# Decode attention with adaLN: softmax rows turned by VectorE instead of TensorE, the second batch's scores placed behind the first value product, and w1 loaded in two halves

## The chip, the core and the metric

One core of one Trainium2 chip. The metric is device time in microseconds (us) for one execution of the program; the median of three runs is given, and beside it the time of the one execution that the profiler recorded. Engines: PE (TensorE, matmuls; PEld is its weight load), DVE (VectorE), ACT (ScalarE), POOL (GpSimd), and SP (SyncE), which here issues nearly all transfers.

## What is computed

One decode step, 8 batches, one token each, width 512. A conditioning vector gives six modulations. The normalised and modulated token is projected to 32 query heads; groups of 4 heads share one of 8 key/value heads; only the last 2048 of 8192 cached positions count. The result goes through `wo`, a gated residual, a second modulated norm, and a squared-ReLU MLP of width 1792. All of it is f32.

```python
    scores = jnp.einsum("bhqd,bhkd->bhqk", q, k) * (Dh ** -0.5)
    p = _softmax(scores, axis=-1)
    o = jnp.einsum("bhqk,bhkd->bhqd", p, v)
    return (lambda x, *d: x.transpose(*d))(o, 0, 2, 1, 3).reshape(B, Sq, Hq * Dh) @ wo
...
x = A_x
mod = (_silu(c) @ w_mod).reshape(c.shape[0], 6, 1, -1)
sa, ca, ga, sb, cb, gb = (mod[:, 0], mod[:, 1], mod[:, 2], mod[:, 3], mod[:, 4], mod[:, 5])
h = _layernorm(x, axis=-1) * (1 + ca) + sa
x = x + ga * _A_ref(h, A_k_cache, A_v_cache, A_wq, A_wo)
h = _layernorm(x, axis=-1) * (1 + cb) + sb
x = x + gb * _B_ref(h, B_w1, B_b1, B_w2, B_b2)
return x
```

## The kernel before

**Loads.** Four slots in SBUF, each 128 partitions x 32 KB, hold whatever is being read from HBM: `w_mod` and `wq` first, then keys and values, then `wo`, `w1`, `w2`. One K or V load is 4096 KB: four of the eight key/value heads of one batch. The order is fixed by the list `loads` (L104 to L111): K(0,0), K(0,1), K(1,0), V(0,0), K(1,1), V(0,1), K(2,0), V(1,0), and so on: the keys run one batch ahead of the values. A load is issued on SP's queue as soon as a slot is given back by `done`, and `done` is called where the code that last read the slot stands. SP's queue is in order. Issue and use are therefore tied to the order of the PE program: `scores(b, t)` gives back a K slot, `weighted(b, t)` a V slot.

**Scores.** K arrives with positions on partitions. `turn` (L284) transposes it in place on DVE in 32x32 squares, four pieces of 128x2048 a slot. `scores` (L294) then runs 16 matmuls against `qb`, a table with each query in a block of its own (`fill`, L271), and gathers one batch's scores in a PSUM tile S of 128x512.

**Softmax.** `rows` copies S to SBUF on ACT (L306) and permutes its partition rows by 16 matmuls against slices of the identity (L310) into a second PSUM tile. `maximum` (L320) takes each partition's maximum on DVE; in `exponent` four small matmuls (L326) share it among the partitions of one head, DVE takes the minimum of the four negated results (L330), and ACT exponentiates with a running sum (L333). `divisor` adds the sums over partitions by a matmul (L345) and inverts (L347, `rz`). `spread` writes the scaled probabilities four times over (L355, ACT); `turn_p` transposes them by PE in four parts n = 0 to 3, using two PSUM tiles in turn (L365), and masks them into `pT` on DVE (L366).

**Values.** `weighted(b, t)` (L378) multiplies `pT` into a V slot with 32 matmuls; ACT copies the result out (L388); `gather` adds the heads' parts into `oT` (L396 to L407).

**Order.** The loop at L409 writes out the order for every engine by hand: the softmax of batch b-1 lies between the four turns of K(b,0). All engines run their own instructions in order and meet at semaphores. For each b: maximum, turn, exponent and gather, turn, divisor and spread, turn, two `turn_p`, turn, two `turn_p`, `scores(b,0)`, `weighted(b-1,0)`, the four turns of K(b,1), `scores(b,1)`, `rows(b)`, `weighted(b-1,1)`.

**End.** `wo` in three loads (16, 12 and 4 of its 32 rows) is multiplied at L453; residual and norm give `h2T` (L143); then `w1` (one load, L485, 4 chunks of 4 matmuls), squared ReLU, a turn (`rT`), `w2` (four loads, L505) and the output.

Of the kernel before, what the change touches and what calls it, by code (L numbers as in the profile page):

```python
# [18 lines left out]
def tile_adaln_cached_attention_mlp(  # L19
# [51 lines left out]
    def load(key):  # L71
# [19 lines left out]
        elif kind == "w1":  # L91
            pieces = [(0, w1.rearrange(r_kc, p=P))]
        else:
            v = w2.rearrange("(p c) n -> p c n", p=P)
            pieces = [(lo, v[:, lo:hi]) for lo, hi in ((0, 8), (8, 12), (12, 13), (13, 14))]
# [31 lines left out]
    ident = consts.tile([P, 2, P], F32, name="ident")  # L127
    make_identity(nc, ident[:, 0, :])
    one = ident[:, 0, :]
    nc.vector.tensor_copy(ident[:, 1, :], one)  # L130
# [42 lines left out]
    def scaled(xm, rstd, add, name):  # L173
# [36 lines left out]
    nc.gpsimd.memset(oT, 0.0)  # L210

# [56 lines left out]
    qrep_b = qrep.rearrange("p x c r b -> p (x c r) b")  # L268

    def fill(b):  # L270
        nc.vector.tensor_mul(  # L271
            qb[b % 2][:, :, :4],
            qrep_b[:, :, b, None].to_broadcast([P, 128, 4]),
            block[:, None, :].to_broadcast([P, 128, 4]),
# [5 lines left out]
    S_, S2_, NM_, PR_, RZ_, PT_, O_ = {}, {}, {}, {}, {}, {}, {}  # L280
# [5 lines left out]
    def scores(b, t):  # L286
# [3 lines left out]
        q = qb[b % 2].rearrange("p n z -> p (n z)")  # L290
# [12 lines left out]
    def rows(b):  # L303

        ss = work.tile([P, 512], F32, name="ss", tag="a")
        nc.scalar.copy(ss, S_.pop(b))  # L306
        S2_[b] = ps_s.tile([P, 4, P], F32, name="s2_ps")
        for a in range(4):
            for j in range(4):
                nc.tensor.matmul(  # L310
                    S2_[b][32 * j : 32 * j + 32, a, :],
                    one[:, a::4],
                    ss[:, P * j : P * j + P],
                    start=True,
                    stop=True,
                )

    def maximum(b):
        mx = work.tile([P, 1], F32, name="mx")
        nc.vector.tensor_reduce(mx, S2_[b].rearrange("p a n -> p (a n)"), axis=AX.X, op=ALU.max)  # L320
        NM_[b] = mx
# [230 lines left out]
```

## Time and profile before

| | |
|---|---|
| median of 3 runs | 400.16 us (399.04 to 400.53) |
| profiled execution | 397.71 us, of it 395.8 us from first to last instruction (the span) |
| mean granted clock of PE | 0.853 |
| busy: PE / DVE / ACT | 274.2 / 195.0 / 47.2 us |
| moved by DMA | 165.18 MB, mean 417 GB/s |
| chain that ended last | DMA 52%, PE 27%, DVE 18% |

The page cuts the span into 40 slices of 9.9 us. A digit is a busy share in tenths; GB/s is what the DMA engines moved in the slice. In a row of instructions the columns are start, duration, engine, line, operation, output<-inputs, shape and count, and in brackets the idle time ahead and what ended it. A row of the grouped view has total busy time, mean ns of one, and idle time with what ended most of it. A row of the DMA issues has the count, KB each and median us from issue to landing.

### The profile page before, as it was taken

The page shows a single profiled execution, that of the slowest core. Times are in us where ns is not written, and L with a number is a line of the kernel's source. Part 1 is how long each engine was busy: PE and PEld are TensorE (multiplying, and loading weights), DVE is VectorE, ACT ScalarE, POOL GpSimd, SP SyncE. Part 2 cuts the span into 40 slices and gives each one's busy share as a digit, 9 for nine tenths or more (in the row PEclk, how much of TensorE's full clock was granted, in tenths as well). Part 3 has the DMA queues.
Part 4 walks back from the last instruction along what each step waited for, and adds up shares of the span by engine and source line. Part 5 has one row for each costly group of instructions (what it writes and reads, how often), then busy time and mean ns, then how long its engine had stood idle before and what let it go on. Part 6 is the DMA issues. An engine that isn't in the chain of part 4 may idle for free.

```text
span 395.8 us, 5381 instructions
## 1 busy us (share of the span) xinstructions
PE 274.2 (69%) x2448; PEld 125.2 (32%) x2448; DVE 195.0 (49%) x186; ACT 47.2 (12%) x95; POOL 4.6 (1%) x11
## 2 busy tenths in 40 slices
PE   0445717859968596859695969596939685988664
PEld 0211301235343224333422343234313433354123
DVE  2320298299084908491848184819281847030022
ACT  1300100030030003000300030003000300032010
POOL 4000000000000000000000000000000000000000
PEclk9986758968986879998868979997888898989889
DMA  8999999998999999999999999999999999999993
GB/s 330 426 434 442 437 431 427 424 422 325 426 442 450 426 424 422 431 429 454 429 425 426 424 426 434 449 431 422 431 422 431 442 426 431 434 429 424 418 422 120
DMA packets 6711, 165.18 MB, mean 417 GB/s; under 512 B 792, under 2 KB 1056, under 8 KB 1312
## 3 DMA queue, kind: packets, MB, share of 16 engines
q1 hardware_dynamic: 6480, 164.69, 97.3%
q8 instruction: 19, 0.31, 0.3%
q10 hardware_dynamic: 144, 0.13, 0.1%
q14 instruction: 4, 0.03, 0.0%
q0 software_dynamic: 64, 0.01, 0.0%
HBM read 164.77 MB, written 0.07 MB: 416 GB/s over the span
## 4 chain that ended last, share of the span: by engine, by line
DMA 52%; PE 27%; DVE 18%; ACT 1%; issue 1%; DVEq 0%; ACTq 0%
DMA slot<-in_A_k_cache_dram 43%; PE s_ps L294 17%; DVE slot L284 17%; DMA slot<-in_B_w_dram 6%; DMA xc_in<-in_xc_dram 3%; PE o_ps L378 3%; PE t_ps L365 2%; PE m_ps L219 2%; PE t_ps L485 1%; PE t_ps L505 1%; PE s_ps L310 1%; ACT prd L355 0%; ACT ss L306 0%; PE m_ps L326 0%; DVE e_sb L149 0%
## 5 line engine op out<-in xcount | busy, mean ns | idle before, releaser
L284 DVE STREAM_TRANSPOSE slot<-slot 128x2048 f32<-128x2048 f32 x64 | 144.2, 2288 | 40.2 <-DMA slot<-in_A_k_cache_dram 40.2
L294 PE MATMUL s_ps<-slot,qb 128*32 128x512 f32 x512 | 121.1, 1092 | 49.6 <-DVE slot L284 48.5
L294 PEld LDWEIGHTS s_ps<-slot,qb 128*32 128x32 f32 x512 | 25.1, 135 | 123.0 <-issue 78.3
L378 PE MATMUL o_ps<-slot,pT 128*32 128x256 f32 x1024 | 59.0, 380 | 0.0
L378 PEld LDWEIGHTS o_ps<-slot,pT 128*32 128x32 f32 x1024 | 39.9, 111 | 24.0 <-issue 9.8
L365 PE MATMUL t_ps<-ident,prd 128*128 128x128 f32 x128 | 30.5, 416 | 21.2 <-ACT prd L355 20.6
L320 DVE TENSOR_REDUCE mx<-s_ps 128x1 f32<-128x512 f32 x8 | 5.5, 691 | 72.9 <-PE s_ps L310 72.9
L365 PEld LDWEIGHTS t_ps<-ident,prd 128*128 128x128 f32 x128 | 23.9, 216 | 25.7 <-ACT prd L355 24.7
L388 ACT COPY o_sb<-o_ps 128x256 f32<-128x256 f32 x16 | 6.0, 372 | 140.2 <-PE o_ps L378 140.2
L355 ACT ACTIVATE prd<-pr,rz 128x512 f32<-128x512 f32 x32 | 20.5, 711 | 17.9 <-DVE rz L347 17.9
L366 DVE TENSOR_TENSOR pT<-t_ps,m4r 128x512 f32<-128x512 f32 x32 | 20.9, 670 | 3.2 <-PE t_ps L365 2.5
L241 PE MATMUL t_ps<-slot,h1T 128*32 128x512 f32 x64 | 12.1, 922 | 9.8 <-DMA slot<-in_A_wq_dram 9.8
L306 ACT COPY ss<-s_ps 128x512 f32<-128x512 f32 x8 | 4.7, 585 | 106.5 <-PE s_ps L294 106.5
L310 PEld LDWEIGHTS s_ps<-ss,ident 128*32 128x32 f32 x256 | 7.0, 139 | 20.8 <-ACT ss L306 20.8
L310 PE MATMUL s_ps<-ss,ident 128*32 128x128 f32 x256 | 8.9, 279 | 5.7 <-ACT ss L306 5.7
L453 PE MATMUL s_ps<-slot,oT 128*32 128x512 f32 x64 | 9.0, 712 | 5.1 <-DMA slot<-in_A_wo_dram 5.1
L253 DVE STREAM_TRANSPOSE qT<-t_ps 128x512 f32<-128x512 f32 x2 | 1.4, 716 | 19.0 <-PE t_ps L241 18.9
L159 PE MATMUL m_ps<-xsum,sel 128*128 128x1 f32 x2 | 0.6, 362 | 14.1 <-DVE xsum L182 14.1
L326 PEld LDWEIGHTS m_ps<-mx,nident 128*128 128x128 f32 x64 | 7.7, 191 | 3.9 <-issue 2.5
L326 PE MATMUL m_ps<-mx,nident 128*128 128x1 f32 x64 | 8.4, 253 | 0.8 <-DVE mx L320 0.8
L241 PEld LDWEIGHTS t_ps<-slot,h1T 128*32 128x32 f32 x64 | 2.8, 159 | 18.8 <-issue 13.4
L219 PE MATMUL m_ps<-slot,cT 128*32 128x384 f32 x64 | 7.3, 625 | 0.0
(90 smaller groups left out, 93.0 us busy)
## 6 DMA issues: line engine op xcount, KB each, us to landing
slot<-in_A_k_cache_dram SPq DMA_DIRECT2D x16, 4096.0 KB, 22.2
slot<-in_A_v_cache_dram SPq DMA_DIRECT2D x16, 4096.0 KB, 26.3
slot<-in_A_wq_dram SPq DMA_DIRECT2D x2, 4096.0 KB, 31.9
slot<-in_w_mod_dram SPq DMA_DIRECT2D x2, 3072.0 KB, 14.0
slot<-in_A_wo_dram SPq DMA_DIRECT2D x1, 4096.0 KB, 22.2
slot<-in_B_w_dram SPq DMA_DIRECT2D x1, 3584.0 KB, 24.3
slot<-in_A_wo_dram SPq DMA_DIRECT2D x1, 3072.0 KB, 24.3
slot<-in_B_w_dram SPq DMA_DIRECT2D x1, 2048.0 KB, 25.7
```

Of the source, the lines that this page charges most:

```text
L219: nc.tensor.matmul(pm[i][32 * q : 32 * q + 32, : 3 * P].rearrange("p (m n) -> p m n", m=3), cT[:, kc, :], wm[:, 3 * i : 3 * i + 3, q, :], ...
L241: nc.tensor.matmul(pq[t][32 * x : 32 * x + 32, :], hT[:, kc, :], w[:, 2048 * t + 512 * x : 2048 * t + 512 * x + 512], start=(kc == 0), sto ...
L284: nc.vector.transpose(k, k)
L294: nc.tensor.matmul(S_[b][32 * x : 32 * x + 32, :].rearrange("p (j i) -> p j i", i=8), q[:, n : n + 32], k[:, :, c, :, x], start=(t == 0 an ...
L310: nc.tensor.matmul(S2_[b][32 * j : 32 * j + 32, a, :], one[:, a::4], ss[:, P * j : P * j + P], start=True, stop=True,)
L326: nc.tensor.matmul(pw[:, w : w + 1], nident[:, 32 * w : 32 * w + P], NM_[b], start=True, stop=True)
L355: nc.scalar.activation(d, pr[:, 4 * n : 4 * n + 4, :, None].to_broadcast([P, 4, 32, 4]), AF.Copy, scale=RZ_[b][0])
L365: nc.tensor.transpose(pp[:, P * i : P * i + P], d[:, i].rearrange("p i u -> p (i u)"), one)
L366: nc.vector.tensor_mul(PT_[b][:, 4 * n : 4 * n + 4, :].rearrange("p j (q x r) -> p (j q) x r", x=4, r=8), pp.rearrange("p (q x r) -> p q x ...
L378: nc.tensor.matmul(o[32 * g : 32 * g + 32], PT_[b][:, j, 64 * q + t : 64 * q + 64 : 2], v[:, 2 * q : 2 * q + 2, j, :], start=(j < 2), stop ...
L388: nc.scalar.copy(O_[b][:, t], o)
L453: nc.tensor.matmul(wo_ps[32 * (i % 4) : 32 * (i % 4) + 32, :], oT[:, i, :], slot(("wo", i // 16), D)[:, i % 16, :], start=(i < 4), stop=(i ...
```

## The change

- The partition rows of S are permuted by two square transposes on DVE (`s1`, `s2`) in place of ACT's copy and 16 matmuls. The permutation differs, so `qb`, `pT`, the masks and the order of the V rows follow it.
- The maximum is shared by DVE alone: into one column of a zeroed 128x32 tile, a square transpose, a maximum over four groups, a scaled broadcast, a square transpose back.
- `rows`, `maximum` and `exponent` of batch b follow each other directly behind `scores(b,1)`; `divisor` and `spread` stand behind the first turn of the next batch, and each pair of `turn_p` one turn sooner than before.
- For b = 1 alone `weighted(0,0)` stands ahead of `scores(1,0)`.
- `w1` is loaded by two DMAs of two chunks each.
- The sum over partitions uses a table `same` in place of `sel`.

```diff
         elif kind == "w1":
-            pieces = [(0, w1.rearrange(r_kc, p=P))]
+            v = w1.rearrange(r_kc, p=P)
+            pieces = [(0, v[:, :2]), (2, v[:, 2:])]
...
+    m16 = consts.tile([P, 4, 4, REP], F32, name="m16")
+    nc.vector.tensor_copy(m16, m4[:, None, :, None].to_broadcast([P, 4, 4, REP]))
+    own = consts.tile([P, 4, 8], F32, name="own")
+    nc.vector.tensor_reduce(own, one.rearrange("p (x q r) -> p x r q", x=4, q=4), axis=AX.X, op=ALU.add)
+    same = consts.tile([P, 4, 4, 8], F32, name="same")
+    nc.vector.tensor_copy(same, own[:, :, None, :].to_broadcast([P, 4, 4, 8]))
...
+    mx = consts.tile([P, 32], F32, name="mx")
+    nc.gpsimd.memset(mx, 0.0)
...
     def rows(b):
-        ss = work.tile([P, 512], F32, name="ss", tag="a")
-        nc.scalar.copy(ss, S_.pop(b))
-        S2_[b] = ps_s.tile([P, 4, P], F32, name="s2_ps")
-        for a in range(4):
-            for j in range(4):
-                nc.tensor.matmul(
-                    S2_[b][32 * j : 32 * j + 32, a, :], one[:, a::4], ss[:, P * j : P * j + P],
...
+        s1 = work.tile([P, 4, 16, 8], F32, name="s1", bufs=1)
+        nc.vector.transpose(
+            s1.rearrange("p a j r -> p j a r"), S_.pop(b).rearrange("p (j i) -> p j i", i=32)
+        )
+        s2 = work.tile([P, 512], F32, name="s2")
+        nc.vector.transpose(s2, s1.rearrange("p a j r -> p (a j r)"))
+        S2_[b] = s2
 
     def maximum(b):
-        mx = work.tile([P, 1], F32, name="mx")
-        nc.vector.tensor_reduce(mx, S2_[b].rearrange("p a n -> p (a n)"), axis=AX.X, op=ALU.max)
-        NM_[b] = mx
+        nc.vector.tensor_reduce(mx[:, 0:1], S2_[b], axis=AX.X, op=ALU.max)
+        mt = work.tile([P, 32], F32, name="mt", bufs=1)
+        nc.vector.transpose(mt, mx)
+        mq = work.tile([P, 8], F32, name="mq", bufs=1)
+        nc.vector.tensor_reduce(mq, mt.rearrange("p (q r) -> p r q", q=4), axis=AX.X, op=ALU.max)
+        mb = work.tile([P, 4, 8], F32, name="mb", bufs=1)
+        nc.vector.tensor_scalar(mb, mq[:, None, :].to_broadcast([P, 4, 8]), -SCALE, None, op0=ALU.mult)
+        nm = work.tile([P, 32], F32, name="nm")
+        nc.vector.transpose(nm, mb.rearrange("p q r -> p (q r)"))
+        NM_[b] = nm
 
     def exponent(b):
-        pw = bank()
-        for w in range(4):
-            nc.tensor.matmul(
-                pw[:, w : w + 1], nident[:, 32 * w : 32 * w + P], NM_[b], start=True, stop=True
-            )
-        nm = work.tile([P, 1], F32, name="nm")
-        nc.vector.tensor_reduce(nm, pw[:, :4], axis=AX.X, op=ALU.min)
...
     def weighted(b, t):
...
-        for j in range(16):
-            for q in range(2):
-                g = (2 * j + q) % 4
-                nc.tensor.matmul(
-                    o[32 * g : 32 * g + 32],
-                    PT_[b][:, j, 64 * q + t : 64 * q + 64 : 2],
-                    v[:, 2 * q : 2 * q + 2, j, :],
...
+        for m in range(32):
+            n, q, u = m // 8, m // 2 % 4, m % 2
+            nc.tensor.matmul(
+                o[32 * (m % 4) : 32 * (m % 4) + 32].rearrange("p u d -> p (u d)"),
+                PT_[b][:, n, 2 * q + t, 2 * u : 2 * u + 2, :].rearrange("p u r -> p (u r)"),
+                v[:, 256 * m : 256 * m + 256],
...
     for b in range(B + 1):
-        if b > 0:
-            maximum(b - 1)
         if b < B:
             turn(b, 0, 0)
         if b > 0:
-            exponent(b - 1)
+            divisor(b - 1)
+            spread(b - 1)
         if b > 1:
             gather(b - 2)
         if b < B:
             turn(b, 0, 1)
         if b > 0:
-            divisor(b - 1)
-            spread(b - 1)
-        if b < B:
-            turn(b, 0, 2)
-        if b > 0:
             turn_p(b - 1, 0)
             turn_p(b - 1, 1)
         if b < B:
-            turn(b, 0, 3)
+            turn(b, 0, 2)
         if b > 0:
             turn_p(b - 1, 2)
             turn_p(b - 1, 3)
         if b < B:
+            turn(b, 0, 3)
+        if b == 1:
+            weighted(0, 0)
+        if b < B:
             scores(b, 0)
-        if b > 0:
+        if b > 1:
             weighted(b - 1, 0)
...
             scores(b, 1)
             rows(b)
+            maximum(b)
+            exponent(b)
```

PE, from the second half of batch 0's scores to batch 0's second value product; before (slot_83 and slot_84 hold K(1,0) and V(0,0); slot_81 and slot_82 hold first batch 0's keys, then K(1,1) and V(0,1)):

```order
L294 MATMUL s_ps<-slot_82,qb_137 32x512 x16
L310 MATMUL s_ps<-ss,ident 32x128 x16
L326 MATMUL m_ps<-mx,nident 128x1 x4
L345 MATMUL m_ps<-z,sel 128x1
L365 MATMUL t_ps<-ident,prd 128x128 x16
L294 MATMUL s_ps<-slot_83,qb_138 32x512 x16
L378 MATMUL o_ps<-slot_84,pT 32x256 x32
L294 MATMUL s_ps<-slot_81,qb_138 32x512 x16
```

The same place on PE in the changed kernel (its lines have other numbers: L297 are scores, L344 the divisor, L366 the transposes, L378 the value product):

```order
L297 MATMUL s_ps<-slot_82,qb_138 32x512 x16
L344 MATMUL m_ps<-z,same 128x1
L366 MATMUL t_ps<-ident,prd 128x128 x16
L378 MATMUL o_ps<-slot_84,pT 32x256 x32
L297 MATMUL s_ps<-slot_83,qb_139 32x512 x16
L297 MATMUL s_ps<-slot_81,qb_139 32x512 x16
```

The 16 + 4 matmuls of L310 and L326 are gone, and the value product on slot_84 has moved ahead of the scores on slot_83.

SP, the loads K(1,1), V(0,1), K(2,0), V(1,0), before, with the semaphores that each waits for (DMAHW: the load that filled the slot before, PE and DVE: its readers):

```order
L81 DMA slot_81<-in_A_k_cache_dram 128x1x8192 [waits DMAHW5_49,DVE_49,PE_49]
L81 DMA slot_82<-in_A_v_cache_dram 128x1x8192 [waits DMAHW6_49,DVE_49,PE_49]
L81 DMA slot_83<-in_A_k_cache_dram 128x1x8192 [waits DMAHW7_49,DVE_49,PE_49]
L81 DMA slot_84<-in_A_v_cache_dram 128x1x8192 [waits DMAHW0_49,PE_49]
L81 DMA slot_81<-in_A_k_cache_dram 128x1x8192 [waits DMAHW1_49,DVE_49,PE_49]
```

And in the changed kernel:

```order
L81 DMA slot_81<-in_A_k_cache_dram 128x1x8192 [waits DMAHW5_49,DVE_49,PE_49]
L81 DMA slot_82<-in_A_v_cache_dram 128x1x8192 [waits DMAHW6_49,DVE_49,PE_49]
L81 DMA slot_84<-in_A_k_cache_dram 128x1x8192 [waits DMAHW0_49,PE_49]
L81 DMA slot_83<-in_A_v_cache_dram 128x1x8192 [waits DMAHW7_49,DVE_49,PE_49]
L81 DMA slot_81<-in_A_k_cache_dram 128x1x8192 [waits DMAHW1_49,DVE_49,PE_49]
```

K(2,0) now goes to the slot that V(0,0) gives back, and V(1,0) to that of K(1,0).

DVE, around batch 0's maximum, before (slot_83 is K(1,0)):

```order
L320 TENSOR_REDUCE mx<-s_ps 128x1
L284 STREAM_TRANSPOSE slot_83<-slot_83 128x2048
L330 TENSOR_REDUCE nm<-m_ps 128x1
L284 STREAM_TRANSPOSE slot_83<-slot_83 128x2048
L347 RECIPROCAL rz<-m_ps 128x1
L284 STREAM_TRANSPOSE slot_83<-slot_83 128x2048
L366 TENSOR_TENSOR pT<-t_ps,m4r 128x512 x2
```

And in the changed kernel (L287 is the turn, L313 and the row ahead of it the two transposes of the score rows, L348 `rz`, L367 the masking into `pT`):

```order
L313 STREAM_TRANSPOSE s_300<-s_298 128x512
L318 TENSOR_REDUCE mx<-s_300 128x1
L320 STREAM_TRANSPOSE mt<-mx 128x32
L322 TENSOR_REDUCE mq<-mt 128x8
L324 TENSOR_SCALAR mb<-mq 128x32
L326 STREAM_TRANSPOSE nm<-mb 128x32
L287 STREAM_TRANSPOSE slot_83<-slot_83 128x2048
L348 RECIPROCAL rz<-m_ps 128x1
L287 STREAM_TRANSPOSE slot_83<-slot_83 128x2048
L367 TENSOR_TENSOR pT<-t_ps,m_130 128x512 x2
```

The whole chain down to the shared maximum stands ahead of the first turn, and `rz` and the first two masking steps each behind one turn fewer.

56 lines of the change are left out of this document (22 added, 34 removed).

## The prediction

> **What bounds the kernel now.** I read the page's slices first, then stretches of the timeline, then the queue that issues the loads. The page's slices (9.9 us each):
>
> ```profile
> DMA  8999999998999999999999999999999999999993
> GB/s 330 426 434 442 437 431 427 424 422 325 426 442 450 426 424 422 431 429 454 429 425 426 424 426 434 449 431 422 431 422 431 442 426 431 434 429 424 418 422 120
> ```
>
> The transfers set the time: from slice 2 to slice 39 they move 418 to 454 GB/s, with one hole, slice 10 (325). The head is short because transfers are starting, the last slice is arithmetic alone. So only two things can shorten this kernel: closing the hole, and shortening what follows the last bytes. The hole by stretches (columns: length, busy time of PE, PEld, DVE, ACT, POOL, clock, DMA share, GB/s):
>
> ```profile
> 94.00:95.00 1.00, 1.00 (x8) 0.28 (x4) 1.00 (x1) 0.00 (x0) 0.00 (x0) 1.00 0.76 328
> 95.00:96.00 1.00, 1.00 (x14) 0.52 (x10) 1.00 (x2) 0.00 (x0) 0.00 (x0) 1.00 0.23 98
> 96.00:97.00 1.00, 1.00 (x25) 1.00 (x20) 1.00 (x1) 0.00 (x0) 0.00 (x0) 1.00 0.00 0
> 80.00:100.00 20.00, 16.10 (x121) 9.27 (x125) 18.54 (x14) 3.71 (x7) 0.00 (x0) 0.74 0.91 372
> 100.00:360.00 260.00, 196.06 (x1818) 93.87 (x1813) 138.32 (x116) 34.15 (x65) 0.00 (x0) 0.86 1.00 431
> ```
>
> Against 431 GB/s, 372 over 20 us is 20 x 59/431 = 2.7 us lost; by the page's slices 9.9 x (428 - 325)/428 = 2.4. I take **2.6**. The queue says why:
>
> ```profile
> 75.26 0.54 SPq L81 DMA_DIRECT2D slot<-in_A_v_cache_dram  x1
> 95.89 0.54 SPq L81 DMA_DIRECT2D slot<-in_A_k_cache_dram  x1
> ...
> 129.99 0.54 SPq L81 DMA_DIRECT2D slot<-in_A_k_cache_dram  x1
> ```
>
> Between 75.26 and 95.89 nothing is issued: all four slots are held. The load of 75.26 runs out near 95.0, and what 95.89 asks for flows about 1.5 us later. I write K20 for batch 2's first keys, V00 for batch 0's first values.
>
> **The change: the hole.** What holds the slots before 95.89:
>
> ```profile
> 67.61 7.59 PE L294 MATMUL s_ps<-slot,qb 128*32 128x512 f32 x32 [2.07 <-DVE slot L284]
> 77.69 2.30 DVE L284 STREAM_TRANSPOSE slot<-slot 128x2048 f32<-128x2048 f32 x1
> 82.17 0.13 DVE L347 RECIPROCAL rz<-m_ps 128x1 f32<-128x1 f32 x1
> 83.17 4.00 PE L365 MATMUL t_ps<-ident,prd 128*128 128x128 f32 x16 [1.89 <-ACT prd L355]
> 88.01 1.25 DVE L366 TENSOR_TENSOR pT<-t_ps,m4r 128x512 f32<-128x512 f32 x2
> 88.19 7.62 PE L294 MATMUL s_ps<-slot,qb 128*32 128x512 f32 x32 [1.02 <-issue]
> 95.48 3.79 PE L378 MATMUL o_ps<-slot,pT 128*32 128x256 f32 x64
> 109.95 2.31 DVE L284 STREAM_TRANSPOSE slot<-slot 128x2048 f32<-128x2048 f32 x1 [0.73 <-DMA slot<-in_A_k_cache_dram]
> ```
>
> The value product waits at 95.48 only for the scores of 88.19 in PE's order; its last operand is ready at 88.01 + 1.25 = 89.3. After the change it goes first and gives V00's slot to K20. Its new time hangs on the new chain on DVE, which has no rows; the nearest ones are
>
> ```profile
> L284 DVE STREAM_TRANSPOSE slot<-slot 128x2048 f32<-128x2048 f32 x64 | 144.2, 2288 | 40.2 <-DMA slot<-in_A_k_cache_dram 40.2
> L320 DVE TENSOR_REDUCE mx<-s_ps 128x1 f32<-128x512 f32 x8 | 5.5, 691 | 72.9 <-PE s_ps L310 72.9
> L253 DVE STREAM_TRANSPOSE qT<-t_ps 128x512 f32<-128x512 f32 x2 | 1.4, 716 | 19.0 <-PE t_ps L241 18.9
> L143 DVE STREAM_TRANSPOSE rT<-relu 128x448 f32<-128x448 f32 x1 | 0.9, 941 | 0.0
> L143 DVE STREAM_TRANSPOSE cT<-e_sb 128x128 f32<-128x128 f32 x1 | 0.4, 405 | 0.0
> L330 DVE TENSOR_REDUCE nm<-m_ps 128x1 f32<-128x4 f32 x8 | 1.2, 152 | 8.9 <-PE m_ps L326 8.9
> ```
>
> s1 (128x512, reordered): 0.72 by L253, 941 x 512/448 = 1.08 by rT, which also reorders; I take 1.08. s2: 2288/4 = 0.57, at most 1.08; take 0.6. The maximum 0.69. The two 32-wide turns: cT and rT lie on a line of 0.19 us plus 1.68 ns an element, so 0.24 each (0.13 to 0.41). The two small steps on 8 and 32 columns: 0.2 and 0.16 (from L330 upwards). Sum 3.2, with seven handovers of 0.03 us **3.4 us**; ends 2.5 and 4.4.
>
> Scores end at 75.2, so the chain ends at 78.6 (the first turn begins 0.9 later than 77.69). Then four turns at 2.22 us, rz 0.1 and four L366 steps 2.7: the last L366 ends at 88.1, the last turn at 90.3. PE's 16 transposes hide among them, as from 83.17. One value product takes at most the 3.79 us of 95.48, and its last quarter, 0.9 us, needs the last L366; so it ends near 89.0: **K20 is issued at 89.0 instead of 95.89**, 4.5 us before the latest useful moment (95.0 - 1.5). The hole closes: -2.6 us.
>
> Does it reopen? Without a pause the four following loads (4096 KB or 4.19 MB at 431 GB/s, 9.7 us each; the row stands below) end at 95.0 + 38.9 = 133.9, so K30 must be issued by 132.4 (before: 129.99). New: scores 90.3; four turns to 99.3; scores 7.6 to 106.9; chain 3.4 to 110.3 (before, this turn began at 109.95, waiting for keys); four turns, rz, L366 and gather 12.4 to 122.7; scores 7.6 to 130.3. Spare 2.1 us, with the chain in it twice: it holds up to a chain of 4.4. For later batches DVE idles 40.2 us for keys, and that covers the added 2.6 us of DVE work a batch.
>
> **At nothing.** PE's L310 and L326 and the copy L306 vanish from stretches in which PE waits for turns; that only frees a V slot sooner while two loads are queued. `fill`, L366, the score and value products keep their counts and sizes under new layouts; uncovered, a tenth on L366 would be 0.27 us a batch. The setup's extra copies lie ahead of the first keys, under slices 2 to 5 of transfers (426 to 442 GB/s). The last w2 piece now waits for the wait counter of the first wo load, which lands by 364, long before that piece is wanted; only the output stands behind it on SP.
>
> **The tail.**
>
> ```profile
> 357.98 5.49 SPq L98 DMA_DIRECT2D slot<-in_B_w_dram  x5
> 364.09 3.64 PE L453 MATMUL s_ps<-slot,oT 128*32 128x512 f32 x32 [1.55 <-DMA slot<-in_A_wo_dram]
> 371.31 5.34 PE L453 MATMUL s_ps<-slot,oT 128*32 128x512 f32 x32 [3.58 <-DMA slot<-in_A_wo_dram]
> 381.32 0.40 DVE L143 STREAM_TRANSPOSE h2T<-h_sb 128x128 f32<-128x128 f32 x1
> 382.38 4.57 PE L485 MATMUL t_ps<-slot,h2T 128*32 128x448 f32 x32 [1.09 <-DMA slot<-in_B_w_dram]
> 389.24 3.27 PE L505 MATMUL t_ps<-slot,rT 128*32 128x128 f32 x112 [1.95 <-DVE rT L143]
> slot<-in_A_k_cache_dram SPq DMA_DIRECT2D x16, 4096.0 KB, 22.2
> ...
> slot<-in_B_w_dram SPq DMA_DIRECT2D x1, 3584.0 KB, 24.3
> ...
> slot<-in_B_w_dram SPq DMA_DIRECT2D x1, 2048.0 KB, 25.7
> ...
> slot<-in_B_w_dram SPq DMA_DIRECT2D x2, 256.0 KB, 27.7
> ```
>
> All of this moves up 2.6 us with the transfers. Beyond that: h2T is ready at 381.72, w1 holds L485 until 382.38. Half of w1 (1792 KB, 1.83 MB) lands 4.3 us sooner, the other half where all of it landed, under L485's own first half. So 0.6 us goes; what is late next is h2T. It hangs on wo's second half, 5.34 us where the first took 3.64:
>
> ```profile
> 364.00:367.00 3.00, 2.91 (x28) 1.12 (x32) 0.00 (x0) 0.00 (x0) 0.00 (x0) 1.00 1.01 429
> 372.00:373.00 1.00, 1.00 (x12) 0.36 (x8) 0.00 (x0) 0.00 (x0) 0.00 (x0) 0.50 1.24 528
> ```
>
> The granted clock was 1.00 in the first and 0.50 in the second, after 3.58 us of waiting. After the change the last softmax ends sooner (one turn and L326 fewer in it), so PE idles some 4.5 us before wo's *first* half; if that one runs at 0.50 and 5.3 us, the wait before the second half shrinks from 3.6 to 1.9 us, and a wait of 1.55 us kept the clock at 1.00 (364.09). Then the second half takes 3.64: up to 1.7 us more. The end is then bound by the last w2 piece: issued near 363.1 (the SP row's end, 363.47, less one issue), landed 27.7 later, 390.8, against 392.3 where L505 needed it (389.24 + 3.27, less its last eight of 112). So the tail gives 0.6 with a slow second half and at most 1.4 with a fast one; I take **1.3**.
>
> [...] Here the w2 pieces of 2 MB down to 256 KB land 25.7 to 27.7 us after issue in an unbroken stream, so I add nothing for the halves.
>
> **Sum.** 2.6 + 1.3 = 3.9 us. The profiled execution took 397.71 (span 395.8) and would take 393.8; the runs' median is 400.16, 2.45 longer, and I take the same 3.9 off it: **396.3**. A measurement of this kernel tells about 0.5% (2 us) from no change.
>
> **Rivals.**
> *Slow tail (0.25).* wo's second half or L485 still runs at 0.50: for it speaks that both did before (L485 took 4.57), against it the shorter wait. Sum 2.6 + 0.6 = 3.2: 396.9. [...]
>
> *The hole comes back before K30 (0.12).* The chain is nearer 5 us; each further us costs 2 us there (it counts twice). At 5.0 us 1.2 comes back: 2.6 - 1.2 + 0.6 = 2.0, so 398.2. The 1.08 of rT speaks for dear reordered turns, the 0.57 of L284 against.
>
> *The change doesn't do what it says (0.08).* The value product is held by something I place early (PE's transposes wait for L366 to empty their two buffers), K20 goes out near 95 as before, only 0.6 of w1 is left: 399.5.
>
> *Slower (0.06).* The same chain, but s1 and s2 cost near 3 us each because of their reordered sides: a chain of about 8 us. K30 then stalls 2 x (8 - 4.4) = 7.2 us, less 2.6 + 0.6: 404. It decides from 6.0 us, where 3.2 us come back; no row of 512 columns is dearer than 1.08, which speaks against it.
>
> **How the numbers follow.** Forecast 0.45, with the rivals above 0.96; 0.04 for a better end. Faster by over 0.5% (below 398.2): 0.45 + 0.25 + 0.04 and a third of the K30 case, 0.78; within 0.5%: the rest of that case and the one that does nothing, 0.15; slower 0.07. The range goes from 395.4 (both upper bounds, 2.7 + 1.4, and 0.6 for the runs' spread) to 398.4 (the K30 case).
>
> **What would show it.** Slice 10 above 415 GB/s; K's third issue after 75 near 89 instead of 95.89; the first turn of batch 1 about 78.6; s1 near 1.1 us; K30 issued by 132; no DMA wait before L485; wo's second half near 3.7 us. The forecast is wrong if zero rates stand anywhere between 90 and 140, or if the final bytes come later than 388.5.

## The result, and the profile after

| | before | after |
|---|---|---|
| median | 400.35 us (4 runs, 399.04 to 401.02) | 395.25 us (4 runs, 393.83 to 395.58) |
| profiled execution | 397.71 us (span 395.8) | 395.58 us (span 393.7) |
| mean granted clock of PE | 0.853 | 0.827 |
| busy: PE / DVE / ACT | 274.2 / 195.0 / 47.2 us | 258.6 / 213.5 / 42.0 us |

The ratio of the times is 0.987, with a 95% interval of 0.9835 to 0.9905: 5.1 us faster. The forecast was 396.3 us, with a range from 395.4 to 398.4; the time lies 0.15 us below that range. The two profiled executions are only 2.1 us apart, the medians 5.1. Where the other 3 us are is the main question of what follows. (Profiled was the longest of the four executions of the changed kernel; the kernel before was profiled in one of its shorter ones.)

The page's slices of the changed kernel (9.8 us each, GB/s):

```profile
GB/s 330 430 429 431 443 433 429 436 429 426 424 429 431 433 431 436 433 428 428 429 429 424 439 429 439 429 421 433 431 433 428 434 426 431 433 428 426 415 421 109
```

Slice 10 went from 325 to 426 GB/s. No slice between 2 and 39 is below 415. The same stretches of the timeline as before the change (the last two columns are DMA share and GB/s):

```profile
80.00:100.00 20.00, 16.25 (x120) 6.77 (x124) 19.57 (x14) 2.93 (x5) 0.00 (x0) 0.87 0.98 421
100.00:360.00 260.00, 180.97 (x1562) 86.94 (x1554) 153.93 (x153) 29.88 (x59) 0.00 (x0) 0.82 1.00 431
388.00:389.00 1.00, 1.00 (x27) 0.93 (x23) 0.00 (x0) 0.00 (x0) 0.00 (x0) 0.52 0.01 4
```

The stretch from 80 to 100 moves 421 GB/s instead of 372, so of the 2.7 us lost there 20 x 10/431 = 0.5 are left: 2.3 us came back. From 100 to 360 us the rate is 431 in both. SP's queue, with the third and the sixth issue as the ones to look at:

```profile
75.21 0.54 SPq L81 DMA_DIRECT2D slot<-in_A_v_cache_dram  x1
89.08 0.54 SPq L81 DMA_DIRECT2D slot<-in_A_k_cache_dram  x1
...
129.06 0.54 SPq L81 DMA_DIRECT2D slot<-in_A_k_cache_dram  x1
```

K20 is issued at 89.08 (forecast 89.0, before 95.89), K30 at 129.06 (forecast 130.3). The timeline of the new chain on DVE and of the first value product:

```profile
75.22 0.72 DVE L309 STREAM_TRANSPOSE s<-s_ps 128x512 f32<-128x512 f32 x1 [6.60 <-PE s_ps L297]
75.97 0.71 DVE L313 STREAM_TRANSPOSE s<-s 128x512 f32<-128x512 f32 x1
76.78 0.69 DVE L318 TENSOR_REDUCE mx<-s 128x1 f32<-128x512 f32 x1
...
78.34 2.27 DVE L287 STREAM_TRANSPOSE slot<-slot 128x2048 f32<-128x2048 f32 x1
...
85.35 3.67 PE L378 MATMUL o_ps<-slot,pT 128*32 128x256 f32 x64
```

From 75.22 to 78.34 are 3.12 us (forecast 3.4). The tail of the changed kernel:

```profile
361.77 5.25 PE L453 MATMUL s_ps<-slot,oT 128*32 128x512 f32 x32 [5.12 <-DMA slot<-in_A_wo_dram]
368.99 3.64 PE L453 MATMUL s_ps<-slot,oT 128*32 128x512 f32 x32 [1.97 <-DMA slot<-in_A_wo_dram]
377.45 0.40 DVE L142 STREAM_TRANSPOSE h2T<-h_sb 128x128 f32<-128x128 f32 x1
378.11 5.18 PE L485 MATMUL t_ps<-slot,h2T 128*32 128x448 f32 x32
385.60 4.88 PE L505 MATMUL t_ps<-slot,rT 128*32 128x128 f32 x112 [1.96 <-DVE rT L142]
```

Here it went as forecast up to `h2T`, the tile that the product of `w1` needs (ready at 377.45 + 0.40 = 377.85): the first half of `wo` is the slow one now (5.25), the wait before the second shrank from 3.58 to 1.97, and that half takes 3.64. L485 starts 4.27 us sooner than before (382.38). But then L485 and L505 take 5.18 and 4.88, where the profile of before shows 4.57 and 3.27: 2.22 us of the 4.27 are spent again, and 2.05 are left (the spans differ by 2.1). By stretches of 2 us:

```profile
374.00:376.00 2.00, 0.41 (x3) 0.35 (x3) 1.31 (x6) 0.49 (x2) 0.00 (x0) 0.83 1.00 425
376.00:378.00 2.00, 2.00 (x10) 0.64 (x10) 0.93 (x4) 0.26 (x1) 0.00 (x0) 0.50 1.07 457
378.00:380.00 2.00, 2.00 (x16) 0.59 (x16) 0.00 (x0) 0.00 (x0) 0.00 (x0) 0.50 0.96 407
386.00:388.00 2.00, 2.00 (x48) 1.84 (x42) 0.00 (x0) 0.00 (x0) 0.00 (x0) 0.50 0.43 169
```

PE is busy for 0.41 us of two, and then the granted clock is 0.50 for most of L485, and again for most of L505.

### The profile page after: what moved, and what is told of

Read it like the earlier page. It is cut to its first block, busy times and chain, and to the rows that moved or that the text cites. A ratio compares the mean times of both kernels' runs of the same rounds, so it can differ in the third digit from the quotient of the medians.

```text
span 393.7 us, 4788 instructions
## 1 busy us (share of the span) xinstructions
PE 258.6 (66%) x2128; PEld 114.7 (29%) x2128; DVE 213.5 (54%) x226; ACT 42.0 (11%) x87; POOL 4.7 (1%) x12
## 4 chain that ended last, share of the span: by engine, by line
DMA 52%; PE 23%; DVE 22%; ACT 1%; issue 1%; DVEq 0%; ACTq 0%
DMA slot<-in_A_k_cache_dram 43%; DVE slot L287 20%; PE s_ps L297 15%; DMA slot<-in_A_wo_dram 7%; DMA xc_in<-in_xc_dram 3%; PE m_ps L221 2%; PE t_ps L485 1%; PE t_ps L505 1%; PE s_ps L453 1%; PE o_ps L378 1%; PE t_ps L366 1%; DVE pT L367 0%; PE t_ps L480 0%; PE m_ps L167 0%; ACT sq L163 0%
## 5 line engine op out<-in xcount | busy, mean ns | idle before, releaser
L287 DVE STREAM_TRANSPOSE slot<-slot 128x2048 f32<-128x2048 f32 x64 | 144.0, 2283 | 43.5 <-DMA slot<-in_A_k_cache_dram 43.3
L297 PE MATMUL s_ps<-slot,qb 128*32 128x512 f32 x512 | 121.1, 1095 | 69.6 <-DVE slot L287 68.7
L297 PEld LDWEIGHTS s_ps<-slot,qb 128*32 128x32 f32 x512 | 23.3, 136 | 147.0 <-issue 80.2
L378 PE MATMUL o_ps<-slot,pT 128*32 128x256 f32 x1024 | 59.6, 380 | 1.0 <-DMA slot<-in_A_v_cache_dram 1.0
L378 PEld LDWEIGHTS o_ps<-slot,pT 128*32 128x32 f32 x1024 | 47.0, 112 | 27.6 <-issue 18.2
L366 PE MATMUL t_ps<-ident,prd 128*128 128x128 f32 x128 | 27.4, 376 | 16.7 <-ACT prd L356 9.8
L309 DVE STREAM_TRANSPOSE s<-s_ps 128x512 f32<-128x512 f32 x8 | 5.7, 717 | 54.2 <-PE s_ps L297 54.2
L366 PEld LDWEIGHTS t_ps<-ident,prd 128*128 128x128 f32 x128 | 20.6, 192 | 22.3 <-ACT prd L356 22.1
L332 ACT ACTIVATE pr<-s,nm 128x512 f32<-128x512 f32 x8 | 5.8, 722 | 142.6 <-DVE nm L326 142.6
L367 DVE TENSOR_TENSOR pT<-t_ps,m 128x512 f32<-128x512 f32 x32 | 20.2, 668 | 0.7 <-PE t_ps L366 0.6
L274 DVE TENSOR_TENSOR qb<-qrep,block 128x512 f32<-128x512 f32 x8 | 8.8, 1097 | 2.2 <-ACT qrep L266 2.2
L344 PE MATMUL m_ps<-z,same 128*128 128x1 f32 x16 | 3.3, 273 | 9.2 <-ACT pr L332 9.2
L404 DVE TENSOR_TENSOR og<-m_ps,m 128x128 f32<-128x128 f32 x8 | 2.2, 271 | 9.1 <-PE m_ps L396 9.1
```

The source lines that it names most:

```text
L274: nc.vector.tensor_mul(qb[b % 2][:, :, :, :REP], qrep_b[:, :, None, :, b].to_broadcast([P, 32, 4, REP]), block[:, None, :, None].to_broadc ...
L287: nc.vector.transpose(k, k)
L297: nc.tensor.matmul(S_[b][32 * x : 32 * x + 32, :].rearrange("p (j i) -> p j i", i=8), q[:, n : n + 32], k[:, :, c, :, x], start=(t == 0 an ...
L332: nc.scalar.activation(pr.rearrange("p j (a i) -> p j a i", a=4), S2_.pop(b).rearrange("p (a j i) -> p j a i", a=4, i=8), AF.Exp, bias=NM_ ...
L366: nc.tensor.transpose(pp[:, P * i : P * i + P], d[:, i].rearrange("p i u -> p (i u)"), one)
L367: nc.vector.tensor_mul(PT_[b][:, n].rearrange("p q j (x r) -> p q (j x) r", r=REP), pp.rearrange("p (y q r) -> p q y r", y=16, r=REP), m16 ...
```

## The experiments

The theory at the start: both parts of the forecast hold, and the time beyond it lies in the tail, where PE's clock differs from execution to execution. The rival: the new softmax saves time of its own. Each ratio is against runs of the kernel before on the same chip, whose medians were 399.9 (29 runs), 400.1 (29) and 400.04 (11) us.

### The parts by themselves

The kernel before unchanged (`before_again`):

> The kernel before, unchanged, for a second profile. The change gained 5.1 us between medians but only 2.1 us between the two profiled executions (395.8 and 393.7 us of span). Theory A (the granted clock in the tail is a matter of phase, and the first profile of before was a fast draw): this execution's span is 396.5 to 399, transfers run at 430 to 432 GB/s between 100 and 360 us with the hole again worth 2.4 to 2.8 us, and what is longer lies behind 370 us, in matmuls at a granted clock of 0.50. Theory B (the hole itself differs from run to run): the hole is 4 us or more. Theory C (the transfers are slower in most executions of before): the rate between 100 and 360 us is 428 GB/s or less.

Measured: 399.4 us (10 runs, 397.07 to 400.81), ratio 0.999 [0.9964, 1.0017]. One kernel spreads over 3.7 us. The profiled execution (399.01, span 397.2) moves 372 GB/s from 80 to 100 us and 431 from 100 to 360, as the first one did; what is longer is the product of `w2`, 4.78 us for 3.27. Theory A holds. Over all its runs here the kernel before falls into two groups, 397.05 to 397.97 and 399.01 to 401.7 us, and only about one execution in six is in the shorter one. A median says little about how far each group moved, so the experiments below are also compared shortest with shortest.

`first_alone`: the kernel before with only the value product moved.

```diff
+        if b == 1:
+            weighted(0, 0)
         if b < B:
             scores(b, 0)
-        if b > 0:
+        if b > 1:
             weighted(b - 1, 0)
```

> Before, with one edit: in batch 1 the first value product stands ahead of the scores. Theory A: the third K load is issued near 90 us in place of 95.9, slice 10 is above 415 GB/s, and the time is 2.6 us below before (ratio 0.9935). Rival (the softmax on DVE is what paid): the hole stays at 2 us or more, because in the old softmax the value product is not ready before 94, and the time is within 0.5 us of before.

Measured: 396.67 us (7 runs, 396.47 to 399.27), ratio 0.9933 [0.9903, 0.9962]. K20 is issued at 91.07 and the stretch from 80 to 100 moves 421 GB/s: one line closes the hole. The ratio meets the forecast of 0.9935 partly by luck: five of the seven executions lie between 396.47 and 396.68, only some 0.7 us below the shortest of before (397.21), and the median of before lies in its longer group. Its tail:

```profile
363.24 5.34 PE L455 MATMUL s_ps<-slot,oT 128*32 128x512 f32 x32 [4.25 <-DMA slot<-in_A_wo_dram]
370.34 3.64 PE L455 MATMUL s_ps<-slot,oT 128*32 128x512 f32 x32 [1.76 <-DMA slot<-in_A_wo_dram]
381.45 4.59 PE L487 MATMUL t_ps<-slot,h2T 128*32 128x448 f32 x32 [1.92 <-DMA slot<-in_B_w_dram]
```

The second half of `wo` comes at 370.34, only 1.0 us ahead of before (371.31), though the hole is as closed as in the changed kernel (368.99). The experiment `old_softmax` below shows where the rest went.

`halves_alone`: the kernel before with only the split of `w1`.

```diff
-            pieces = [(0, w1.rearrange(r_kc, p=P))]
+            v = w1.rearrange(r_kc, p=P)
+            pieces = [(0, v[:, :2]), (2, v[:, 2:])]
```

> Before, with one edit: w1 in two halves. By the prediction's sum 0.6 us less (ratio 0.9985), which these rounds may not tell from none; L485 begins within 0.1 us of h2T and no DMA wait stands ahead of it. Rival (two transfers cost more than one): L485 or L505 begin later against the end of h2T, and the time is 0.5 to 1 us above before.

Measured: 396.84 us (11 runs, 396.17 to 398.99), ratio 0.9933 [0.9911, 0.9954]: by the ratio 2.7 us, where the forecast had 0.6 for this edit. Shortest against shortest it is 1.0 (396.17 against 397.21); the rest is that the shorter group now holds six of eleven executions. The profiled one, the longest (398.99), shows the product of `w1` without a wait and, up to 385 us, at a granted clock of 0.50 all the same:

```profile
381.73 5.09 PE L486 MATMUL t_ps<-slot,h2T 128*32 128x448 f32 x32
```

No price of the two smaller loads shows: the product starts 0.26 us behind `h2T` (381.07 + 0.40 = 381.47), and the shortest execution is 1.0 us below that of before.

`not_first`: the changed kernel with the value product back behind the scores.

```diff
-        if b == 1:
-            weighted(0, 0)
-        if b > 1:
+        if b > 0:
             weighted(b - 1, 0)
```

> The changed kernel, with the scores of batch 1 put back ahead of the first value product. Theory A: scores from 90 to 97.5, the third K load is issued at 97.5, later than the 95.9 of before, the hole is 4 us (transfers stop from 95 to 99), and the time is 4 us above the changed kernel, so about 1 us below before. Rival (softmax on DVE gives most of the gain): within 1.5 us of the changed kernel.

Measured: 399.36 us (12 runs, 397.5 to 399.96), ratio 0.9977 [0.9959, 0.9995]. SP's queue and the stretch from 80 to 100:

```profile
97.64 0.54 SPq L81 DMA_DIRECT2D slot<-in_A_k_cache_dram  x1
```

```profile
80.00:100.00 20.00, 13.87 (x99) 7.84 (x102) 19.64 (x14) 2.56 (x4) 0.00 (x0) 0.77 0.83 345
```

Without the moved product the DVE chain makes the hole larger (345 GB/s against 372; K20 at 97.64 against 95.89). In the changed kernel the move is worth 399.36 - 395.25 = 4.1 us, as expected. Without it the softmax on DVE costs time: `halves_alone`, which differs from this kernel by that softmax, took 2.5 us less.

### The tail, with PE kept busy and with w1 whole

In these kernels PE runs extra matmuls on constants in the tail, whose results nobody reads; the work of the kernel is the same. The text shows `after_warm`; in `before_warm` and `halves_warm` the numbers are 0, 12, 2, 2, 1 and 6.

```diff
+    spare = ps_o.tile([P, 2, P], F32, name="o_ps")
+    def busy(n):
+        for _ in range(n):
+            nc.tensor.matmul(spare[:, 0, :], one, one, start=True, stop=True)
+    busy(14)
...
+        if i == 15:
+            busy(6)
...
+            busy(2)
...
+    busy(2)
...
+    busy(1)
...
+    busy(6)
```

`before_warm`:

> Before, with matmuls of no use (identity by identity into an unread PSUM tile) in PE's waiting times behind the last attention product: 12 between the two parts of wo, 2 + 2 + 1 in the norm, 6 ahead of w2. Theory A (the clock's phase in the tail makes the spread and most of what halves_alone gained): granted clock 1.00 from 364 us on, L453's second part 3.7 us, L485 3 us, L505 3.3 us; the time is 395.5 to 397, and its runs lie within 1.5 us. Rival (the spread is in the transfers): the runs still lie over 3 us apart and the median stays above 398.

Measured: 398.15 us (12 runs, 397.22 to 398.7), ratio 0.9956 [0.9938, 0.9973]. That is a miss: more was expected. Its tail shows why:

```profile
363.61 5.34 PE L463 MATMUL s_ps<-slot,oT 128*32 128x512 f32 x32 [1.66 <-DMA slot<-in_A_wo_dram]
371.75 3.64 PE L463 MATMUL s_ps<-slot,oT 128*32 128x512 f32 x32
381.90 6.16 PE L499 MATMUL t_ps<-slot,h2T 128*32 128x448 f32 x32 [1.45 <-DMA slot<-in_B_w_dram]
```

The second half of `wo` now takes 3.64 us, but the first takes 5.34, and with the 12 extra matmuls behind it the second starts only at 371.75, without a wait for its load; in the four profiles of the kernel before it starts between 370.85 and 371.31. PE still stands 1.45 us for `w1`, and the product of `w1` then takes 6.16 us, at a granted clock of 0.50 from 382 to 387 us.

`halves_warm`, the same with `w1` in halves:

> before_warm with w1 in two halves. Theory A: what the halves gained alone was mostly the clock's phase; with a steady clock both kernels end when the last w2 piece lands, so within 0.6 us of before_warm. Rival (the halves are worth 3 us in themselves, through the wait ahead of L485): 2.5 to 3 us below before_warm.

Measured: 397.01 us (12 runs, 396.32 to 398.34), ratio 0.9942 [0.9917, 0.9967], 1.1 below `before_warm`; expected was no more than 0.6. The product of `w1`:

```profile
379.98 1.71 PE L500 MATMUL t_ps<-slot,h2T 128*32 128x448 f32 x16
382.23 1.71 PE L500 MATMUL t_ps<-slot,h2T 128*32 128x448 f32 x16 [0.54 <-DMA slot<-in_B_w_dram]
```

At a granted clock of 1.00 (380 to 384 us) it takes 2 x 1.71 us. So the halves save most of the wait (0.54 us for 1.45), and in this execution the clock stays at 1.00. That the saved wait is what keeps it there is not shown: in `halves_alone`, and below in `after_warm` and `old_softmax`, the same product has no wait ahead of it and takes 4.87 to 5.87 us.

`after_warm`:

> The changed kernel with the same useless matmuls in the tail (14 ahead of wo, 6 between its parts, 2 + 2 + 1, 6). Theory A: clock 1.00 from 356 us on, the end is set by the last w2 piece; 393.0 to 394.0, 1.3 to 2.2 us below the changed kernel, 2.6 below before_warm, and the runs within 1 us. Rival: no gain over the changed kernel's 395.25.

Measured: **394.05 us** (6 runs, 393.84 to 394.43), ratio 0.9857 [0.9827, 0.9886], the fastest of all kernels here, and within 0.6 us from run to run. It lies 1.2 us below the changed kernel, just short of the expected 1.3, and the clock isn't at 1.00 throughout (0.50 from 378 to 380 us). Its tail:

```profile
361.48 3.64 PE L463 MATMUL s_ps<-slot,oT 128*32 128x512 f32 x32 [1.75 <-DMA slot<-in_A_wo_dram]
368.70 3.64 PE L463 MATMUL s_ps<-slot,oT 128*32 128x512 f32 x32 [2.04 <-DMA slot<-in_A_wo_dram]
377.41 4.87 PE L499 MATMUL t_ps<-slot,h2T 128*32 128x448 f32 x32
384.76 1.96 PE L520 MATMUL t_ps<-slot,rT 128*32 128x128 f32 x64 [0.60 <-DMA slot<-in_B_w_dram]
387.12 1.80 PE L520 MATMUL t_ps<-slot,rT 128*32 128x128 f32 x48 [0.40 <-DMA slot<-in_B_w_dram]
```

Here the product of `w2` waits for its last pieces. The bound that the forecast gave for the tail is real: it holds once PE is fast enough to reach it, as here (waits of 0.60 and 0.40 us).

`after_whole`, the changed kernel with `w1` in one load:

```diff
-            v = w1.rearrange(r_kc, p=P)
-            pieces = [(0, v[:, :2]), (2, v[:, 2:])]
+            pieces = [(0, w1.rearrange(r_kc, p=P))]
```

> The changed kernel with w1 in one transfer. By the prediction's tail (h2T at 377.9 in the profile after, w1 as a whole landed about 379.6): L485 begins near 379.7 in place of 378.2, and the time is 1.5 us above the changed kernel, or 0 to 3 us if the clock's phase decides. Rival (the halves are worth 3 us in themselves): 3 us above.

Measured: 397.2 us (12 runs, 394.85 to 398.49), ratio 0.9922 [0.9894, 0.995], so the halves are worth 2.0 us in the changed kernel by the medians, and 1.0 shortest against shortest (394.85 against 393.83). In its tail:

```profile
376.94 0.40 DVE L141 STREAM_TRANSPOSE h2T<-h_sb 128x128 f32<-128x128 f32 x1
...
379.78 5.67 PE L484 MATMUL t_ps<-slot,h2T 128*32 128x448 f32 x32 [2.87 <-DMA slot<-in_B_w_dram]
```

`h2T` is ready at 377.34, and `w1` holds the product until 379.78. In the kernel before, the same gap was 0.66 us (381.72 to 382.38): `h2T` moves up further than the transfers do, since `wo`'s second half takes 3.64 us at a granted clock of 1.00 (369 to 372 us), where the profile of before has 5.34 at 0.50 (372 to 374), and then the whole `w1` is what is late.

### The chain, the old softmax, and the kernel before twice more

`chain_slow` is `after_warm` with four more maxima (0.69 us each, into a tile that nobody reads) in the DVE chain of each batch.

```diff
+        late = work.tile([P, 1], F32, name="late")
+        for _ in range(4):
+            nc.vector.tensor_reduce(late, S2_[b], axis=AX.X, op=ALU.max)
```

> after_warm with four more maximum steps of 0.69 us (results unused) in DVE's chain behind each batch's scores: the chain grows from 3.1 to 5.9 us. By the prediction's rule (the chain stands twice ahead of K30, and elsewhere DVE's idle time covers it): the third K load goes from 89.1 to 91.9 us, still without a hole there; K30 is issued near 134.7 in place of 129.1, a hole of 2 to 3 us near 134, none later; the time is 2 to 3 us above after_warm's 394.05. Rival 1 (all covered): within 0.5 us of after_warm. Rival 2 (every batch pays): more than 6 us above.

Measured: 396.03 us (4 runs, 395.97 to 396.26), ratio 0.9918 [0.9886, 0.995], 1.98 above `after_warm`. K20 is issued at 92.22, K30 at 134.46, and right behind that the transfers pause (window, then busy times, clock, DMA share, GB/s):

```profile
132.00:134.00 2.00, 2.00 (x12) 0.57 (x8) 2.00 (x2) 0.00 (x0) 0.00 (x0) 1.00 0.91 393
134.00:136.00 2.00, 2.00 (x41) 1.78 (x37) 2.00 (x2) 0.00 (x0) 0.00 (x0) 1.00 0.39 131
136.00:138.00 2.00, 2.00 (x37) 1.61 (x33) 0.43 (x1) 0.08 (x1) 0.00 (x0) 1.00 1.01 410
```

This is the mechanism of the rival *the hole comes back before K30*. Its price is 2 us for a chain of 5.8 (75.15 to 80.96); the rival's own rule, 2 us for each us above 4.4, gives 2.8, since the forecast placed K30 1.2 us too late and so made the spare too small. The change itself has 129.06 there, and no pause. Maxima in the six later batches cost little or nothing: the chain is 2.7 us longer in each, and the whole kernel only 2.

`old_softmax` is the kernel before with the moved product, the halves and the extra matmuls (6 ahead of `wo`, 12 between its parts): all of the change but the softmax on DVE.

> Before, with the first value product ahead of the scores, w1 in halves and the useless matmuls in the tail, so after_warm but for the softmax, which stays on PE and ACT. Theory A (turns on DVE are worth nothing in time, the order and the halves are all): within 0.5 us of after_warm, 393.6 to 394.6. Rival (freeing PE and ACT is worth something by itself): 1 us or more above after_warm.

Measured: 395.76 us (6 runs, 395.25 to 396.5), ratio 0.9908 [0.988, 0.9937], 1.7 above `after_warm`. The theory had the new softmax at nothing; here it fell, and the rival stood. The tail:

```profile
363.14 3.64 PE L466 MATMUL s_ps<-slot,oT 128*32 128x512 f32 x32 [0.26 <-DMA slot<-in_A_wo_dram]
370.36 3.64 PE L466 MATMUL s_ps<-slot,oT 128*32 128x512 f32 x32 [0.71 <-DMA slot<-in_A_wo_dram]
379.63 5.87 PE L502 MATMUL t_ps<-slot,h2T 128*32 128x448 f32 x32
```

Both halves of `wo` land 1.7 us later than in `after_warm` (363.14 and 370.36 against 361.48 and 368.70), although the rates up to 360 are the same within 1 GB/s (421 and 430 against 422 and 431; 1 GB/s over 260 us is 0.6 us of transfers). `first_alone` lags behind the changed kernel in the same way (363.24 and 370.34 against 361.77 and 368.99).

By their times, the traces show why. The program's own instructions are loaded too, in packets of 16 KB on queue q8, while the keys and values flow. The pages of all kernels with the old softmax count 19 such packets (first row, `old_softmax`), those of all kernels with the new one 17 (second row, `after_warm`); up to 362 us it is 17 against 15:

```profile
q8 instruction: 19, 0.31, 0.3%
q8 instruction: 17, 0.28, 0.3%
```

The new softmax needs fewer instructions on PE: 2128 matmuls and as many weight loads on the changed kernel's page, 2448 of each on the page before. A load of keys or values arrives in 16 shares, each with a semaphore update of its own, and has landed when the last share has (in the kernel before, K20's last share comes at 109.9 us and the turn that waits for it starts at 109.95). By these updates the shares of the load that lands at 28 us come within 0.7 us of each other in the kernel before and within 0.8 in the changed one. Behind the first instruction packet (32 us) one share comes over 1 us after the others, behind each further packet one more share: in the kernel before each such packet puts one share 1.2 to 1.5 us back (the few packets of 8 KB on queue q14 put one back too, by 0.5 and 1.0 us). The loads themselves still land every 9.7 us, until the ninth packet falls on a share that was late already: in `old_softmax` it goes out at 208.9, and the loads around it land at 204.5 and 215.7, 1.5 us late. DVE's turns, which wait for these keys, show it (19.4 us from the first row to the second, 21.0 to the third):

```profile
185.07 2.31 DVE L287 STREAM_TRANSPOSE slot<-slot 128x2048 f32<-128x2048 f32 x1 [0.34 <-DMA slot<-in_A_k_cache_dram]
204.51 8.89 DVE L287 STREAM_TRANSPOSE slot<-slot 128x2048 f32<-128x2048 f32 x4 [5.51 <-DMA slot<-in_A_k_cache_dram]
225.46 2.31 DVE L287 STREAM_TRANSPOSE slot<-slot 128x2048 f32<-128x2048 f32 x1 [1.86 <-DMA slot<-in_A_k_cache_dram]
```

The seventeenth packet does it again: in `old_softmax` at 357.4 (loads land at 351.7 and 363.0), in `first_alone` at 356.2 (351.8 and 363.1). In `after_warm` the ninth packet goes out at 234.1, and the seventeenth at 387.8, when `wo` and `w1` have long landed. So `first_alone` is 2.4 us ahead of the kernel before up to the load at 351.8 (354.2 before), as the closed hole promises, and 0.9 from the next one on (363.1 against 364.0). In the kernel before the shares come together again at the hole: at 97.4 they are 1.8 us apart, at 109.9 fifteen of the sixteen lie within 0.4 us. The count begins anew there, and the step (245.8 to 257.1) is at the ninth packet from there, 249.0. The changed kernel has its ninth packet at 235.3 and its step from 233.8 to 244.7. No run changed the number of instructions and nothing else, so the cause is read from the times and not tested.

With PE kept busy, the parts of the change can be read one after another: 398.15 (`before_warm`), 397.01 with the halves, 395.76 with the moved product as well (`old_softmax`), 394.05 with the new softmax as well (`after_warm`). That is 1.1, 1.3 and 1.7 us; the extra matmuls aren't placed alike in all four (12 between the parts of `wo` in the first two, 6 and 12 in the third, 14 and 6 in the fourth).

The kernel before twice more, for its profile alone (`before_p2`, `before_p3`):

> The kernel before once more, for a profile of an execution near its median of 400. Theory A: whatever its time, the queue's issues up to 340 us lie within 0.5 us of the other two profiles of before, and time over 397.7 is found in L453, L485 and L505 at a granted clock of 0.50. Rival: the issues are late by 2 us or more before 340 us.

> As before_p2: a further profile of before, read in the same way.

Measured: 400.59 and 400.33 us. The tail of the first:

```profile
371.29 5.07 PE L453 MATMUL s_ps<-slot,oT 128*32 128x512 f32 x32 [3.58 <-DMA slot<-in_A_wo_dram]
...
381.05 0.40 DVE L143 STREAM_TRANSPOSE h2T<-h_sb 128x128 f32<-128x128 f32 x1
...
382.36 5.92 PE L485 MATMUL t_ps<-slot,h2T 128*32 128x448 f32 x32 [1.35 <-DMA slot<-in_B_w_dram]
...
390.58 4.93 PE L505 MATMUL t_ps<-slot,rT 128*32 128x128 f32 x112 [1.95 <-DVE rT L143]
```

And that of the second:

```profile
371.25 6.27 PE L453 MATMUL s_ps<-slot,oT 128*32 128x512 f32 x32 [3.57 <-DMA slot<-in_A_wo_dram]
...
383.07 5.05 PE L485 MATMUL t_ps<-slot,h2T 128*32 128x448 f32 x32
...
390.44 4.81 PE L505 MATMUL t_ps<-slot,rT 128*32 128x128 f32 x112 [1.96 <-DVE rT L143]
```

Between 90 and 340 us their loads are issued within 0.3 us of the first profile, and no more than 0.8 us behind `before_again`: the rival falls. In all four profiles of the kernel before, the second half of `wo` starts between 370.85 and 371.31. What makes one execution 3 us longer than another lies behind it, almost all of it in the lengths of three products. These two, near the median, have all three slow; the execution on which the forecast was worked out, 397.71, had L485 at 4.57 and L505 at 3.27. It was among the shortest.

## Why the forecast was right in kind and missed in size

**The hole: right, but it does not reach the tail alone.** K20's time was met within 0.1 us (partly by luck: the value product follows PE's transposes at 85.35 and takes its full 3.67 us, where the forecast had only its last quarter behind the last L366), K30's within 1.3, and the gain is 2.3 us for 2.6 (the stretch's rate, and `wo`'s second half 371.31 to 368.99). Undoing the move opens the hole again (`not_first`); doing it alone closes it (`first_alone`). But "all of this moves up 2.6 us with the transfers" holds only together with the new softmax: with the move alone `wo`'s second half comes 1.0 us sooner. That the term came out nearly right in the changed kernel is partly luck.

**The chain: right in sum.** 3.12 us for 3.4. s1 was taken dearer than it is (717 ns for 1.08 us), s2 cheaper (711 for 0.6). That K30 is the next place at risk, and that the chain counts twice there, `chain_slow` shows.

**At nothing: one point wrong without effect, one not.** `fill` kept its size but went from 655 to 1097 ns; it lies under DVE's waits for keys (43.3 us in the changed kernel). That PE's L310 and L326 vanish was to free "a V slot sooner" and nothing else; `old_softmax` is 1.7 us slower than `after_warm`, and its loads land 1.7 us later (the numbers of extra matmuls differ as well, 6 and 12 against 14 and 6). By the times, some 1.5 us of this is the seventeenth instruction packet (357.4 us in `old_softmax`, between loads that land 11.3 us apart in place of 9.7), which with PE's old instructions falls ahead of `wo`. So the 2.3 us by which `wo` moves up are not the hole's alone.

**The tail: signs right, size carried over to an execution of another kind.** The signs named for it came: no DMA wait on PE before L485, `wo`'s second half at 3.64 us, 4 GB/s from 388 on. That the shorter wait keeps this half fast is not shown: behind a wait of 2.04 us it takes 3.64 in `after_warm`, behind 2.06 us 5.34 in `chain_slow`. The step that failed is "the runs' median is 400.16, 2.45 longer, and I take the same 3.9 off it". For the profiled execution the forecast said 393.8; the changed kernel's shortest execution, one of four and not profiled, took 393.83, and `after_warm`, whose granted clock is below 1.00 only from 377 to 381 us between 355 and 391, 394.05. The tail's 1.3 us were capped by the last piece of `w2`, and this cap applies where L485 and L505 are fast. In `before_p2` and `before_p3`, near the median of before, L485 runs at 0.50 for most of its time (382 to 387 us in the first) and takes 5.92 and 5.05 us, L505 takes 4.93 and 4.81 (0.50 from 392 to 394 in the first); the cap is out of reach, and the change saves more. Term by term, `before_p2` (400.59) against the changed kernel's profile (395.58):

| | before_p2 | after | saved |
|---|---|---|---|
| `wo`'s second half starts | 371.29 | 368.99 | 2.30 |
| it takes | 5.07 | 3.64 | 1.43 |
| from its end to `h2T` ready | 5.09 | 5.22 | -0.13 |
| from there to the start of L485 | 0.91 | 0.26 | 0.65 |
| L485 and L505 | 10.85 | 10.06 | 0.79 |
| sum | | | 5.04 |

The two times differ by 5.01. So the tail term was mis-sized: 1.43 - 0.13 + 0.65 + 0.79 = 2.74 us where 1.3 was written. Without the cap the prediction's own terms, 0.6 for the wait and 1.7 for `wo`'s second half, come to 2.3. The range's lower end had 0.6 us for the spread of runs, but the kernel before alone spreads over 3.7 to 4.5 us (397.07 to 400.81, 397.21 to 401.7).

**The rivals.** *Slow tail* came true in its condition (L485 at 0.50 from 378 to 382 us) and not in its time, for the same reason: it was slow before as well. *Before K30* and *slower* needed a chain of over 4.4 us; it is 3.12. *Doesn't do what it says* fell with the issue at 89.08.

**A wait's price.** The 0.66 us wait for `w1` was priced at its length. By ratio and medians, removing it is worth 2.7 us alone and 2.0 in the changed kernel; shortest against shortest it is 1.0 in both, and 1.1 between the medians of `before_warm` and `halves_warm`. In the changed kernel `h2T` also moves up further than `w1` does (2.87 us of wait in `after_whole`). The remainder of the 2.7 and 2.0 goes with how many executions fall into the shorter group. Whether the wait itself brings the clock down is open: the product takes 4.57 to 6.16 us behind a wait, and 3.21 (`chain_slow`) to 5.87 without one.

## What to carry to other kernels

Before a difference in one profiled execution is taken off a median, find out which kind of execution it was: profile the kernel two or three times and see which rows change length, since in this tail PE ran the same product at a granted clock of 0.50 or of 1.00 (`w1`: 5.92 us, most of them at 0.50, in `before_p2`, 2 x 1.71 us at 1.00 in `halves_warm`). Where executions fall into two groups, compare the groups and not only the medians. A split of the load ahead of a short wait cost nothing that shows here (`halves_alone` is 1.0 us faster, shortest against shortest). When transfers bound the kernel, look in the issuing queue for the longest gap and ask which instruction holds the slot. And count the instructions: by the times, their own loads delayed those of the data here (1.5 us at 357.4 us in `old_softmax`), so that the move in the order paid in full only when PE had fewer instructions.

## What the runs showed of the hardware

- **The clock fell with PE busy for most of the time.** In `after_warm` the granted clock fell from 1.00 to 0.50 near 377.4 us (0.84 is the mean over 376 to 378), though PE had been busy for 1.59 of the two us ahead of 376 and for 1.93 of the next two:

```profile
374.00:376.00 2.00, 1.59 (x16) 1.23 (x15) 1.08 (x6) 0.49 (x2) 0.00 (x0) 1.00 0.99 419
376.00:378.00 2.00, 1.93 (x15) 0.62 (x18) 0.92 (x3) 0.26 (x1) 0.00 (x0) 0.84 0.98 416
378.00:380.00 2.00, 2.00 (x16) 0.54 (x12) 0.00 (x0) 0.00 (x0) 0.00 (x0) 0.50 1.01 430
```

  What brings it down no run settles.
- **Equal rate, later landing.** Two kernels that move the same GB/s up to 360 us, within 1, had the same load land 1.7 us apart (`old_softmax`, `after_warm`). In the kernel before a 16 KB packet of instructions put one of a load's 16 shares 1.2 to 1.5 us behind, and the ninth, counted from the hole, fell on a share that was late already: the loads around it landed 11.25 us apart in place of 9.7 (in the changed kernel 10.85).
- **The layout of some operands cost time, of others not.** Square turns of 128x512 took 711 to 717 ns, from PSUM with a reordered output (s1) or from SBUF in order (s2); but `rT`, which reads its input across columns, took 941 ns for only 448 columns. The multiply of `fill`, 128x512 as well, went from 655 to 1097 ns with the layout of its operands alone.
